# Thresholded attention into a tanh-shrink layer pair: some DMAs on the GpSimd queue, q prepared two slots sooner, and q of three pairs in four turned by the crossbar

## The chip, the cores and the metric

The kernel runs on one core of a Trainium2 chip. A core has five engines with a queue of instructions each: TensorE (PE; its weight loads are listed apart as PEld), VectorE (DVE), ScalarE (ACT), GpSimd (POOL) and SyncE (SP), which here only issues DMAs. Sixteen DMA engines move data between HBM and the core's memory SBUF and can transpose 2-byte data on the way (the crossbar). TensorE writes to PSUM. Engines run their queues in order and wait for each other by semaphores. The metric is device time in microseconds (us), the median of several runs. A profile is one execution more, recorded by the hardware.

## What is computed

```python
# q, k, v: (8, 8, 576, 64) float32; tau = 0.02; w_in (512, 2048), w_out (2048, 512)
scores = scale * np.matmul(q, k.transpose(0, 1, 3, 2))
thresh = np.max(scores, axis=-1, keepdims=True) - tau
scores = np.where(scores >= thresh, scores, -1000000000.0)
scores = scores - np.max(scores, axis=-1, keepdims=True)
attn = np.exp(scores)
attn = attn / (np.sum(attn, axis=-1, keepdims=True) + 1e-09)
attn_out = np.matmul(attn, v)
x = attn_out.transpose(0, 2, 1, 3).reshape(B * S, H * D)
h = x @ w_in
g = h - np.tanh(h)
out = g @ w_out
```

Attention over 64 (batch, head) combinations of 576 rows each, in which only scores within tau of their row's maximum count, and then two dense layers over the 4608 rows with `h - tanh(h)` between them.

## The kernel before

**Tiles and slots.** Two heads form a pair: 32 pairs `p`, four to a batch. The 2 × 576 query rows of a pair are nine tiles of 128 rows (`TPP = 9`), the ninth made of the last 64 rows of both heads, so there are 288 tiles `i`. The main loop (line 691) runs over slots `s`, one tile a slot. In slot `s` TensorE makes the scores of tile `s + 8` (`AHEAD`), ScalarE bends the scores of tile `s + 5` into `z` (`kink`, `MASK`), ScalarE takes exponentials of tile `s` (`weights`), and TensorE multiplies the weights of tile `s - 2` with v (`attend`, `LAG`). A pair's first scores thus run in slot `first = 9 p - 8`.

**What each tile does.** `scores` multiplies qT with kT and with kS (the same keys with halves swapped, so that the high and low 16-bit parts of q and k meet), 512 and 64 columns each; VectorE scales the result into SBUF and keeps the row maximum (line 336, `sc`). Each pair of tiles gets its thresholds `nb` (line 348). ScalarE makes `z` (363). For the first six pairs TensorE transposes `z` (382); from pair 6 on a crossbar DMA issued by SP does, every second tile for two tiles (line 370, `zT`). ScalarE exponentiates the turned tile (399), and `attend` uses it as weights.

**Preparation of a pair.** `load` (138) fetches k, q and v of a pair, two DMAs each, all on SP's queue (`eng = nc.sync`). `split` (181) makes a 16-bit high and low part of k and of q on GpSimd, three instructions of which the last writes `khl` or `qhl` (188). `split_v` (214) converts v on GpSimd (216 to 221). `turn` (243) transposes: for k, nine TensorE transposes into a PSUM buffer of the pool `ps_big` (which the scores use too), a VectorE copy to `kT` (258), and two GpSimd copies to `kS` (264). For q it does the same without `kS`, except where `q_by_dma(p)` is true: there one crossbar DMA on SP's queue writes qT (247). Before, that is for odd pairs from 9 on and for pair 30, thirteen in all. Buffers: two each for the raw loads, the splits, and kT, kS, qT.

**When it is issued.** `PREP` (642) lists these steps with how many slots ahead of `first` each is placed; the loop from 653 fills a table `plan`, whose steps run at the end of their slot. All is written out in one order, so a step's place fixes its place in every queue it uses:

```python
    PREP = (
        (LDK, lambda p: load(p, "k")),
        (LDK - 1, lambda p: load(p, "q")),
        (LDK - 2, lambda p: load(p, "v")),
        (8, lambda p: split(p, "k")),
        (7, lambda p: split(p, "q")),
        (5, lambda p: turn(p, "k")),
        (4, split_v),
    )
```

`LDK` is 16. The turn of k is moved to 6 slots for odd pairs and 3 for even ones from pair 5 on; q's turn comes 5 slots ahead by DMA, else 2 or 3.

**The layers.** From the second batch on, the two dense layers of the batch before run beside the attention, spread over its slots: `hidden` (493, `psH`), tanh on ScalarE (506), `g` on VectorE (512), `project` (519, `psY`). A finished block of 128 rows is copied to `yo` (532, two buffers) and stored to HBM by a DMA that SP issues (535). Each store is issued only once the next one is ready (lines 726 to 728). The last two blocks of 512 rows and the rest rows of all batches follow after the last tile.

Of the kernel before, what the change touches and what calls it, by code (L numbers as in the profile page):

```python
# [18 lines left out]
def kernel(  # L19
# [11 lines left out]
    nc = tc.nc  # L31
    P = 128

    B, H, S, D = q.shape
# [11 lines left out]
    HPAIR = H // 2  # L46
# [91 lines left out]
    def load(p, t):  # L138
        b, h0 = p // HPAIR, 2 * (p % HPAIR)
        hs = slice(h0, h0 + 2)  # L140
        src = {"k": k, "q": q, "v": v}[t]
        eng = nc.sync
        r = raws[p, t] = raw_pool.tile([P, 10, D], F32, name=f"{t}raw", tag=t)
        n = 8 if t == "v" else 10
        eng.dma_start(
            out=r[:, 0:n, :].rearrange("p (h c) d -> p h (c d)", h=2)[:, :, 0 : 4 * D],
            in_=src[b, hs, 0:512, :].rearrange("h (p c) d -> p h (c d)", c=4),
        )
        rem = src[b, hs, 512:S, :].rearrange("h s d -> s h d")
        if t == "v":  # L150
            eng.dma_start(out=r[0:64, 8:10, :], in_=rem)
        else:
            eng.dma_start(out=r[:, 4, :], in_=rem)
# [84 lines left out]

    def q_by_dma(p):

        return p >= 2 * HPAIR and (p % 2 == 1 or p == 30)

    def turn(p, t):
        hl = hls.pop((p, t))
        if t == "q" and q_by_dma(p):
            m = mats[p, t] = qk_pool.tile([P, W], FP16, name=f"{t}T", tag=t)
            nc.sync.dma_start_transpose(
                out=m.rearrange("p (c r) -> p c r", c=TPP),
                in_=hl.rearrange("p c a d -> p (c a d)"),
            )  # L250
            return
        ps = ps_big.tile([P, W], FP16, name=f"ps_{t}", tag="big")
        for c in range(TPP):
            turn_chunk(
                ps[:, c * P : (c + 1) * P], c, hl[:, c, :, :].rearrange("p a d -> p (a d)")
            )
        m = qk_pool.tile([P, W], FP16, name=f"{t}T", tag=t)
        nc.vector.tensor_copy(out=m, in_=ps)  # L258
        mats[p, t] = m
        if t == "k":  # L260
            sw = qk_pool.tile([P, W], FP16, name="kS", tag="ks")
            for lo, hi in ((0, D), (D, 0)):
                o, i = sw[lo : lo + D, :], m[hi : hi + D, :]
                nc.gpsimd.tensor_copy(out=o, in_=i)  # L264
            mats[p, "ks"] = sw
# [37 lines left out]
    def scores(i):  # L303
# [6 lines left out]
        if hh is None:  # L310
            qrem = REM
            if q_by_dma(p):
                qrem = (slice(512, 640, 2), slice(513, 640, 2))
            for n, kk in enumerate((kT, kS)):
                for dst, srcs in ((main, MAIN), (rem, REM)):
                    for hh in range(2):
                        nc.tensor.matmul(  # L317
                            out=ps[64 * hh : 64 * hh + 64, dst],
                            lhsT=qT[:, qrem[hh]], rhs=kk[:, srcs[hh]],
                            start=(n == 0), stop=(n == 1),  # L320
                        )
        else:
            lhs = qT[:, (5 * hh + t) * P : (5 * hh + t + 1) * P]
            for n, kk in enumerate((kT, kS)):
                for dst, src in ((main, MAIN[hh]), (rem, REM[hh])):
                    nc.tensor.matmul(  # L326
                        out=ps[:, dst], lhsT=lhs, rhs=kk[:, src],
                        start=(n == 0), stop=(n == 1),
                    )
# [157 lines left out]
    gs, stores = {}, []  # L487
# [29 lines left out]
    def project(m, ms, part, ps, last, cols=slice(0, d_model)):  # L517
        for n in range(4 * part, 4 * part + 4):
            nc.tensor.matmul(  # L519
                out=ps, lhsT=gs[m][:, n, ms * P : (ms + 1) * P],  # L520
                rhs=w_out_sb[:, n, cols], start=(n == 0), stop=(n == DF_C - 1),
            )
        if part == 3:
            nc_ = cols.stop - cols.start
            yo = y_pool.tile(
                [P, nc_], F32, name="yo", tag="yo" if nc_ == d_model else f"yo{int(last)}",
                bufs=2 if nc_ == d_model else 1,
            )
            if last:
                nc.scalar.copy(out=yo, in_=ps)  # L530
            else:
                nc.vector.tensor_copy(out=yo, in_=ps)  # L532
            if m < B:
                rows = out[m * S : m * S + MB, :].rearrange("(p c) n -> c p n", c=4)
                stores.append(lambda: nc.sync.dma_start(out=rows[ms], in_=yo))
            else:
                for h in range(2):
                    b = 2 * ms + h
                    eng = nc.scalar if h and nc_ < d_model else nc.sync
                    stores.append(  # L540
                        lambda b=b, h=h, eng=eng: eng.dma_start(
                            out=out[b * S + MB : (b + 1) * S, cols],
                            in_=yo[64 * h : 64 * h + 64, :],
                        )
                    )
# [8 lines left out]
    def layers(m, tail):  # L554
# [9 lines left out]
        def y_step(m, ms, part):  # L564
            if part == 0:

                odd = tail and (m, ms) > (B - 2, 1) and ms % 2 == 0
                pl, tag = (ps_o, "o") if odd else (ps_y, "y")
                ys[m, ms] = pl.tile([P, d_model], F32, name="psY", tag=tag), odd
            ps, odd = ys[m, ms]  # L570
            project(m, ms, part, ps, odd)

        def y_half(h):

            n = d_model // 2
            pl, tag = ((ps_y, "y"), (ps_o, "o"))[h]
            ps = pl.tile([P, n], F32, name="psY", tag=tag)
            for part in range(4):
                project(m, 3, part, ps, h == 0, slice(h * n, h * n + n))
# [48 lines left out]
    def w_load(piece):  # L628
# [12 lines left out]
# [7 lines that stand above are left out]
# [5 lines left out]
    for p in range(1, NPAIR):  # L653
        first = TPP * p - AHEAD
        for d, f in PREP[3 if p == 1 else 0 :]:
            d -= p == 1 and d in (3, 5)
            if d == 5 and p >= 5:
                d = 6 if p % 2 else 3
            plan.setdefault(first - d, []).append(lambda p=p, f=f: f(p))
        d = 5 if q_by_dma(p) else (2) if p >= 5 else 3 - (p == 1)  # L660
        plan.setdefault(first - d, []).append(lambda p=p: turn(p, "q"))

    load(0, "v")
# [27 lines left out]
    for s in range(-AHEAD, NTILE + LAG + 3):  # L691
        p, j = divmod(max(s, 0), TPP)
# [28 lines left out]
        if s == 0:  # L721
            nc.vector.tensor_tensor(
                out=fold, in0=ident_bf[:, 0:64], in1=ident_bf[:, 64:P], op=ALU.add
# [79 lines left out]
```

## Time and profile before

| | us |
|---|---|
| median of 3 runs (lowest, highest) | 535.39 (534.58, 536.02) |
| profiled execution, its own time | 536.14 |
| its span, first to last instruction | 534.4 |
| DMA queue of SP: share of 16 engines | 75.2% |
| v loads on SP: 32 of 256 KB, 32 of 32 KB, median to landing | 3.7 and 3.5 |
| layer stores on SP: 32 of 256 KB, median to landing | 3.1 |
| z turned by the crossbar: 117, median to landing | 3.5 |
| q turned by the crossbar: 13, median to landing | 4.1 |

A row of instructions has the line, the engine, the operation, the tile written `<-` the tiles read, shapes and a count. A number in square brackets is the time that the engine stood idle just before, with what ended it. "SPq" rows are DMA instructions in SP's queue; their duration is that of issuing, not of moving data. The granted TensorE clock was 1.00 throughout. An engine's busy share says little by itself: the share of TensorE is high all through, that of GpSimd highest in the first 66 us, and all but TensorE fall off after 460 us, where only the layers are left.

### The profile page before, as it was taken

The page shows a single profiled execution, that of the slowest core. Times are in us where ns is not written, and L with a number is a line of the kernel's source. Part 1 is how long each engine was busy: PE and PEld are TensorE (multiplying, and loading weights), DVE is VectorE, ACT ScalarE, POOL GpSimd, SP SyncE. Part 2 cuts the span into 40 slices and gives each one's busy share as a digit, 9 for nine tenths or more (in the row PEclk, how much of TensorE's full clock was granted, in tenths as well). Part 3 has the DMA queues.
Part 4 walks back from the last instruction along what each step waited for, and adds up shares of the span by engine and source line. Part 5 has one row for each costly group of instructions (what it writes and reads, how often), then busy time and mean ns, then how long its engine had stood idle before and what let it go on. Part 6 is the DMA issues. An engine that isn't in the chain of part 4 may idle for free.

```text
span 534.4 us, 12822 instructions
## 1 busy us (share of the span) xinstructions
PE 509.6 (95%) x4651; PEld 289.2 (54%) x4651; DVE 423.3 (79%) x1184; ACT 436.7 (82%) x617; POOL 289.5 (54%) x390
## 2 busy tenths in 40 slices
PE   8988899999999998989999999999999999999997
PEld 4666566555555554555555555655555555444444
DVE  5888878989989897889889898899889887554440
ACT  5999899999898988899888989899889999543330
POOL 7999987775737566574727474575747530000000
PEclk9999999999999999999999999999999999999999
DMA  7655547999996999799998999798988995401113
GB/s 203 183 186 146 182 151 186 211 163 200 173 201 146 173 189 201 151 182 195 173 199 140 213 165 210 153 188 185 207 167 178 204 148 110 104 20 41 39 40 79
DMA packets 202687, 85.32 MB, mean 160 GB/s; under 512 B 170240, under 2 KB 195072, under 8 KB 202624
## 3 DMA queue, kind: packets, MB, share of 16 engines
q1 hardware_dynamic: 202032, 84.08, 75.2%
q8 instruction: 36, 0.59, 0.5%
q10 hardware_dynamic: 592, 0.43, 0.3%
q14 instruction: 27, 0.22, 0.1%
HBM read 36.70 MB, written 9.44 MB: 86 GB/s over the span
## 4 chain that ended last, share of the span: by engine, by line
PE 64%; DVE 9%; POOL 9%; DMA 7%; ACT 6%; issue 4%; SPq 0%; POOLq 0%; ACTq 0%; DVEq 0%
PE psY L519 20%; PE psH L493 16%; PE psS L326 14%; DMA qT<-qhl 5%; PE psO L427 3%; PE psHt L493 3%; DVE sc L336 3%; DVE g L512 2%; ACT z L363 2%; POOL kS L264 2%; PE psS L317 2%; DVE yo L532 2%; PE ps_k L235 2%; ACT th L506 1%; POOL w_in_sb L626 1%
## 5 line engine op out<-in xcount | busy, mean ns | idle before, releaser
L336 DVE TENSOR_SCALAR_CACHE_REDUCE sc<-psS 128x576 f32<-128x576 f32 x288 | 214.3, 752 | 40.7 <-PE psS L326 22.0
L363 ACT ACTIVATE z<-sc,nb 128x576 bf16<-128x576 f32 x288 | 217.2, 770 | 32.5 <-DVE nb L348 30.2
L519 PE MATMUL psY<-w_out_sb,g 128*128 128x512 bf16 (+1 forms) x592 | 145.9, 374 | 0.8 <-DVE yo L532 0.8
L264 POOL COPY kS<-kT 64x1152 f16<-64x1152 f16 x62 | 70.8, 1142 | 126.3 <-DVE nb L348 124.7
L399 ACT ACTIVATE pT<-zT 128x1152 f16<-128x1152 bf16 x117 | 135.0, 1154 | 2.0 <-DMA zT<-z 2.0
L493 PE MATMUL psH<-xT,w_in_sb 128*128 128x512 bf16 x480 | 123.3, 379 | 2.3 <-DVE g L512 2.3
L326 PE MATMUL psS<-kT,qT 128*128 128x512 f16 (+1 forms) x512 | 104.4, 285 | 4.6 <-DVE qT L258 1.2
L326 PEld LDWEIGHTS <-qT 128*128 128x128 f16 x1024 | 74.2, 97 | 59.2 <-issue 5.1
L512 DVE SCALAR_TENSOR_TENSOR g<-th,psH 128x512 bf16<-128x512 f32 x128 | 87.4, 683 | 18.9 <-ACT th L506 18.6
L326 PE MATMUL psS<-kS,qT 128*128 128x512 f16 x496 | 101.4, 286 | 0.0
L506 ACT ACTIVATE th<-psH 128x512 f32<-128x512 f32 x128 | 74.7, 583 | 23.7 <-PE psH L493 23.0
L519 PEld LDWEIGHTS <-g 128*128 128x128 bf16 x592 | 51.0, 98 | 56.8 <-issue 2.4
L493 PEld LDWEIGHTS <-w_in_sb 128*128 128x128 bf16 x576 | 49.1, 98 | 57.0 <-issue 4.7
L427 PE MATMUL psO<-vb,pT 128*128 128x65 bf16 x1024 | 53.3, 194 | 0.0
L427 PEld LDWEIGHTS <-pT 128*128 128x128 f16 x1024 | 44.2, 98 | 9.7
L188 POOL TENSOR_TENSOR qhl<-qraw,qhl 128x576 f16<-128x576 f32 x31 | 39.7, 1280 | 2.6
L188 POOL TENSOR_TENSOR khl<-kraw,khl 128x576 f16<-128x576 f32 x31 | 39.7, 1280 | 2.6
L391 ACT ACTIVATE pT<-psZ 128x512 f16<-128x512 bf16 (+1 forms) x54 | 35.0, 651 | 5.0 <-PE psZ L382 4.5
L532 DVE COPY yo<-psY 128x512 f32<-128x512 f32 (+1 forms) x31 | 21.1, 681 | 14.1 <-PE psY L519 12.4
L453 DVE TENSOR_TENSOR osb<-psO,rc 128x256 bf16<-128x256 f32 x64 | 27.1, 424 | 2.2
L420 PE MATMUL psO<-vb,pT 128*128 128x130 bf16 x128 | 28.2, 220 | 0.4
L258 DVE COPY kT<-ps_k 128x1152 f16<-128x1152 f16 x31 | 23.3, 752 | 5.8 <-PE ps_k L235 5.8
(79 smaller groups left out, 516.9 us busy)
## 6 DMA issues: line engine op xcount, KB each, us to landing
vraw<-in_v_dram SPq DMA_DIRECT2D x32, 256.0 KB, 3.7
out_dram<-yo SPq DMA_DIRECT2D x32, 256.0 KB, 3.1
kraw<-in_k_dram SPq DMA_DIRECT2D x31, 256.0 KB, 3.6
qraw<-in_q_dram SPq DMA_DIRECT2D x31, 256.0 KB, 3.7
wt<-in_moe_w_in_dram SPq DMA_DIRECT2D x8, 512.0 KB, 4.7
wt<-in_moe_w_out_dram SPq DMA_DIRECT2D x8, 512.0 KB, 4.4
zT<-z SPq DMA_TRANSPOSE x117, 3.5
kraw<-in_k_dram SPq DMA_DIRECT2D x32, 32.0 KB, 3.5
```

The source lines that it names most:

```text
L188: nc.gpsimd.tensor_tensor(out=hl[:, :, 1, :], in0=x, in1=hl[:, :, 0, :], op=ALU.subtract)
L264: nc.gpsimd.tensor_copy(out=o, in_=i)
L326: nc.tensor.matmul(out=ps[:, dst], lhsT=lhs, rhs=kk[:, src], start=(n == 0), stop=(n == 1),)
L336: nc.vector.tensor_scalar(out=sc, in0=ps[:, lo : lo + S], scalar1=SC, scalar2=None, op0=ALU.mult, op1=ALU.max, accum_out=mx[:, c : c + 1],)
L363: nc.scalar.activation(out=z, in_=sc, func=ACT.Prelu, bias=nb, scale=1.0, alpha=STEEP)
L391: nc.scalar.activation(out=pt[:, off * P : (off + n) * P], in_=ps[:, 0 : n * P], func=ACT.Exp)
L399: nc.scalar.activation(out=pt[:, 0 : n * P], in_=zts.pop(i)[:, 0:n, :], func=ACT.Exp)
L427: nc.tensor.matmul(out=po[:, t - 1 + ab, :], lhsT=pt[:, blk * P : (blk + 1) * P], rhs=vb[:, hh, c, :], start=False, stop=(n == 7), skip_gr ...
L493: nc.tensor.matmul(out=ps, lhsT=w_in_sb[:, c, n * P : (n + 1) * P], rhs=xs[m][:, c, :] if m < B else xR[:, c, :, :], start=(c == 0), stop= ...
L506: nc.scalar.activation(out=th, in_=ps, func=ACT.Tanh)
L512: nc.vector.scalar_tensor_tensor(out=gs[m][:, n, :], in0=th, scalar=-1.0, in1=ps, op0=ALU.mult, op1=ALU.add,)
L519: nc.tensor.matmul(out=ps, lhsT=gs[m][:, n, ms * P : (ms + 1) * P], rhs=w_out_sb[:, n, cols], start=(n == 0), stop=(n == DF_C - 1),)
```

## The change

Four things. v loads from pair 8 on, and the layer stores of the first six blocks of 512 rows, are issued by GpSimd in place of SP. The crossbar turns q of the pairs from 8 on that aren't divisible by four, and of pair 28 (19 pairs: 9, 10, 11, 13, 14, 15, ... 27, 28, 29, 30, 31). For these pairs the splits of k and q are placed 10 and 9 slots ahead in place of 8 and 7, and q's turn 7 in place of 5. The TensorE turn of q in pairs 2 and 4 is placed 2 slots ahead in place of 3. Results don't change.

```diff
@@ -139,7 +139,8 @@
         b, h0 = p // HPAIR, 2 * (p % HPAIR)
         hs = slice(h0, h0 + 2)
         src = {"k": k, "q": q, "v": v}[t]
-        eng = nc.sync
+
+        eng = nc.gpsimd if t == "v" and p >= 2 * HPAIR else nc.sync
         r = raws[p, t] = raw_pool.tile([P, 10, D], F32, name=f"{t}raw", tag=t)
         n = 8 if t == "v" else 10
         eng.dma_start(
@@ -238,7 +239,7 @@
 
     def q_by_dma(p):
 
-        return p >= 2 * HPAIR and (p % 2 == 1 or p == 30)
+        return p >= 2 * HPAIR and (p % 4 != 0 or p == 28)
 
     def turn(p, t):
         hl = hls.pop((p, t))
@@ -532,7 +533,8 @@
                 nc.vector.tensor_copy(out=yo, in_=ps)
             if m < B:
                 rows = out[m * S : m * S + MB, :].rearrange("(p c) n -> c p n", c=4)
-                stores.append(lambda: nc.sync.dma_start(out=rows[ms], in_=yo))
+                eng = nc.gpsimd if m < B - 2 else nc.sync
+                stores.append(lambda: eng.dma_start(out=rows[ms], in_=yo))
             else:
                 for h in range(2):
                     b = 2 * ms + h
@@ -654,10 +656,12 @@
         first = TPP * p - AHEAD
         for d, f in PREP[3 if p == 1 else 0 :]:
             d -= p == 1 and d in (3, 5)
+            if d in (7, 8) and q_by_dma(p):
+                d = d + 2
             if d == 5 and p >= 5:
                 d = 6 if p % 2 else 3
             plan.setdefault(first - d, []).append(lambda p=p, f=f: f(p))
-        d = 5 if q_by_dma(p) else (2) if p >= 5 else 3 - (p == 1)
+        d = 7 if q_by_dma(p) else 3 - (p == 1 or p % 2 == 0 or p >= 5)
         plan.setdefault(first - d, []).append(lambda p=p: turn(p, "q"))
 
     load(0, "v")
```

## The prediction

> **What bounds the kernel now.** I read the engine table first, then the stretch 120 to 450 us alone, then who waits there, then single instructions. First the busy line of the page, and the stretch in which both halves of the kernel run together (start:end, then us busy on each engine, granted clock, DMA share, GB/s).
>
> ```profile
> PE 509.6 (95%) x4651; PEld 289.2 (54%) x4651; DVE 423.3 (79%) x1184; ACT 436.7 (82%) x617; POOL 289.5 (54%) x390
> ...
> 120.00:450.00 330.00, 322.96 (x2976) 181.68 (x2973) 287.99 (x818) 296.27 (x398) 187.00 (x240) 1.00 0.93 179
> ```
>
> TensorE is busy 322.96 of 330 us, ScalarE 90%, VectorE 87%, GpSimd 57%. So TensorE's own work plus its few stalls set the pace here; at most 7.04 us of stalls can be won back. The waits of that stretch (total, times, longest):
>
> ```profile
> POOL kS L264 <- DVE nb L348: 117.8, 22, 10.5
> PEld L317 <- DMA qT<-qhl: 6.1, 7, 1.7
> PE psS L317 <- DMA qT<-qhl: 3.4, 3, 1.4
> ACT pT L399 <- DMA zT<-z: 2.0, 4, 0.9
> PE psS L326 <- DMA qT<-qhl: 0.9, 1, 0.9
> ```
>
> TensorE waits for the crossbar-turned q of a new pair, and for little else. A weight load can wait while the matmul before it still streams, so the PE row counts, not PEld. Two of these stalls, in the timeline of PE, and the second seen from the SP queue:
>
> ```profile
> 206.57 0.43 PE L317 MATMUL psS<-kT,qT 128*64 128x512 f16 x4 [1.23 <-DMA qT<-qhl]
> ...
> 237.48 0.44 PE L317 MATMUL psS<-kT,qT 128*64 128x512 f16 x4 [1.43 <-DMA qT<-qhl]
> ```
>
> ```profile
> 226.13 1.30 SPq L370 DMA_TRANSPOSE zT<-z  x1
> 227.53 0.53 SPq L145 DMA_DIRECT2D kraw<-in_k_dram  x1
> 228.11 0.56 SPq L153 DMA_DIRECT2D kraw<-in_k_dram  x1
> 228.77 0.55 SPq L145 DMA_DIRECT2D qraw<-in_q_dram  x1
> 229.37 0.55 SPq L153 DMA_DIRECT2D qraw<-in_q_dram  x1
> 230.35 1.26 SPq L370 DMA_TRANSPOSE zT<-z  x1
> 231.72 2.02 SPq L247 DMA_TRANSPOSE qT<-qhl  x1
> 233.79 0.57 SPq L145 DMA_DIRECT2D vraw<-in_v_dram  x1
> 234.42 1.33 SPq L151 DMA_DIRECT2D vraw<-in_v_dram  x1
> ```
>
> q's turn is issued at 231.72, behind four loads and a z turn; the chain of waits has it landing 5.72 us later, at 237.44. TensorE stood ready at 237.48 − 1.43 = 236.05, only 4.3 us after the issue. Last, GpSimd, which will have to take the moved DMAs:
>
> ```profile
> 219.75 2.33 POOL L264 COPY kS<-kT 64x1152 f16<-64x1152 f16 x2 [10.52 <-DVE nb L348]
> ...
> 230.60 2.32 POOL L264 COPY kS<-kT 64x1152 f16<-64x1152 f16 x2 [2.94 <-DVE nb L348]
> ...
> 247.95 2.33 POOL L264 COPY kS<-kT 64x1152 f16<-64x1152 f16 x2 [7.07 <-DVE nb L348]
> ```
>
> Two pairs are 18 slots. Each copy waits for VectorE's kT (the row names what VectorE ran last): the even pair's (247.95) with 7.07 us to spare, the odd pair's (230.60) with 2.94.
>
> **What the Trainium skill says.** "DMA: Bandwidth & Descriptors", section "Issuing engines are not separate DMA queues": all issuers share the same 16 engines, and another queue saves only sequencer time. So the v loads and stores don't get cheaper for the engines, whose share is already 0.93; no run here has a GpSimd-issued transfer. The same page, "SWDGE vs HWDGE vs iDMA", says GpSimd's descriptors are written by software on its own cores, so the issue is GpSimd work; its table "Specifications" gives about 1 us to the first byte against 0.6. "SBUF — State Buffer", section "SBUF: two separate sides", warns that VectorE's 2-port modes starve that software; the long VectorE rows here (sc, g, kT) read PSUM, and by the page's "Who interferes with whom" an instruction with at most one SBUF input outside those modes doesn't contend. I count nothing for it.
>
> **The change, part by part.** A slot is 1/36 of a batch; the psY pieces of the chain repeat at 148.22, 207.25, 266.00, 324.06, 381.49, 439.26, so batches take 59.03, 58.75, 58.06, 57.43, 57.77 us and a slot 1.62.
>
> *q's turn two slots sooner.* The q split precedes it on GpSimd; the instruction orders show that GpSimd's compute sequence is the same in both kernels, so q isn't split any sooner: only SP's place moves, from after the k and q loads to before them. At the stall above the split ended at 227.66 (226.38 + 1.28); two slots before 231.72 is 228.5, so data is there, 0.8 us ahead. Landing at 228.5 + 5.7 = 234.2 is before 236.05. All stalls seen are at most 1.43, below 3.2, so all go. Their PE rows: 0.91 (at 119.78, put down there to sc, though the weight load beside it names qT), 1.23, 1.43, 0.70, 0.88: 5.15 us. Cross-check: what batches have above the shortest, 1.60 + 1.32 + 0.63 + 0.34 = 3.89, and 0.91 before them, 4.8. Bounds 3.9 to 7.0; I take **−5.0**. z turns that were behind q's wait no longer; k and q loads go 1.3 us later, with 6 slots to their split.
>
> *Six more pairs by crossbar* (10, 14, 18, 22, 26, 28; 19 against 13). Each drops nine TensorE transposes, which take 0.50 us of the chain ("PE ps_q L235 x9"): 6 × 0.50 = **−3.0**. VectorE's six 755 ns copies go too, off the path, as does one use of a ps_big buffer; bounds −3 to −5. Each adds one SP issue (1.35 us, median) and one crossbar transfer. Its engine time: plain traffic ran at 141 GB/s with share 0.49 in 40 to 54 us, so 46 MB cost about 160 us of the 402 busy (75.2%); the rest over 130 turns is 1.9 us each. Six are 11 us in 330, share 0.93 to 0.96, and 0.98 with the shorter time. Stretches of 14 us show up to 1.11, so the measure isn't full there. Their q is issued 7 slots ahead. Cost 0, bounds 0 to +4 (late z).
>
> *v loads and stores to GpSimd.* 24 pairs × 2 loads + 24 stores: 72 instructions; SP loses 48 × 0.6 + 24 × 0.54 = 42 us of issue. SP waited mostly for ScalarE's z (91.8 us), so this wins nothing itself. GpSimd pays c each. Nearest rows: SP's own 0.54 to 0.65 us; the upper bound is the roughly 2.0 us fixed part in "Anatomy of one DMA — SWDGE (gpsimd) path" of the DMA page, as if the issuer were held for all of it. I take c = 1.0. By the order, five of six DMAs in two pairs stand between the odd pair's kS and the even pair's, one ahead of the odd pair's. Five at 1.0 fit in 7.07 minus the 0.6 by which two pairs shorten, one in 2.9. Loads have 10 slots until the v split; stores aren't issued until a later row block is ready. Cost 0; if the cover goes, 5c − 7.7 us per two pairs, where 7.7 is 6.5 of idle plus 1.2 between kS's end and TensorE's first use (kT turned at 246.52, plus three slots is 251.4; kS ended 250.3).
>
> *q of pairs 2 and 4 one slot later.* Before 66 us GpSimd is 94% busy and sets the pace; TensorE stalled 0.6 us each on VectorE's qT there. Between −1.2 and +2.6; I take 0.
>
> **Sum.** −5.0 − 3.0 = −8.0. The profiled execution took 536.14 (span 534.4): 528.1. It lies 0.75 above the median 535.39, so 527.4; I say **527.5**. Late next is ScalarE, 53 of 57 us in a batch.
>
> **Rivals.**
> 1. *GpSimd late (slower).* Place: kS of even pairs, 12 times. Above c = 1.54 TensorE waits 12 × (5c − 7.7); at c = 1.67 the gain is gone; 1.8 gives 543, 2.0 gives 555. For it: two pairs already hold 17.4 us of GpSimd work in 29, and a v load is 256 pieces of 1 KB. Against it: SP's 0.6 and the page's 1 us.
> 2. *The stalls are replaced.* Fuller DMA engines delay z turns; ScalarE, with 9% to spare, passes it on. For it: zT took up to 6.9 us to land. Against: only 2.0 us of such waits today. It gives back 3 to 6 us: 530.5 to 534.
> 3. *The turn isn't sooner*, because q's split doesn't move on GpSimd and its DMAs delay it: only the −3 stays, 532.4. Against: the 0.8 us to spare at 227.66, and the even pairs' q, split by about 242.8 with three DMAs ahead, against an issue due at 243.1.
>
> **How the numbers follow.** Forecast (525 to 530.5): 0.51. Rivals 2 and 3 together (530.5 to 536): 0.23. Rival 1: 0.26, densest just past its point. No change means within 0.3%, 1.6 us, about what this kernel's timing can tell. Faster: 0.51 + 0.15 = 0.66. Same: 0.08 + 0.01 = 0.09. Slower: 0.25. Range 523 to 541: up to c = 1.76 of rival 1; the likeliest's own is 525 to 530.5.
>
> **What would show it.** qT waits on TensorE near 0; 171 − 54 = 117 ps_q matmuls; GpSimd's DMA issues near 1 us and its idle before even kS 1.5 to 2; zT's median still near 3.5; a batch near 57 us. I am wrong if kS appears as a releaser of TensorE, or if ScalarE waits for zT by more than 5 us.

## The result and the profile after

The changed kernel takes 587.68 us (median of four runs, 581.73 to 590.34) against 535.62 (534.58 to 536.02) for the kernel before: 1.096 times as long, interval 1.0874 to 1.1046. The forecast was 527.5. The profiled execution took 590.34 us, span 588.6, and its TensorE clock was granted at 0.954 on average, against 1.00 before.

First the page of the changed kernel: busy rows, clock, DMA queues, DMA issues (KB of one, median us to landing).

```profile
PE 523.3 (89%) x4535; PEld 293.9 (50%) x4597; DVE 420.6 (71%) x1178; ACT 436.6 (74%) x617; POOL 334.8 (57%) x462
...
PEclk9999999979999799979989799989979799999999
...
q1 hardware_dynamic: 195696, 72.48, 65.1%
q0 software_dynamic: 4608, 13.37, 10.2%
...
vraw<-in_v_dram POOLq DMA_DIRECT2D x24, 256.0 KB, 4.9
out_dram<-yo POOLq DMA_DIRECT2D x24, 256.0 KB, 3.6
```

The change did what it says: a second queue has appeared with 13.37 MB, the 72 new instructions stand on GpSimd (462 against 390), TensorE has 54 weight loads fewer, nine for each of six pairs. (Of its matmul records 116 are gone; 62 of these are missing from this trace, and from e1's below.) TensorE's share fell from 95% to 89%, although its busy time rose, and the clock row has dips at regular distances. The stretch 120 to 450 us, then the two windows around one dip (same columns as in the view before):

```profile
120.00:450.00 330.00, 289.42 (x2470) 160.27 (x2506) 245.09 (x696) 253.93 (x341) 204.02 (x272) 0.93 0.92 161
```

```profile
240.00:251.00 11.00, 10.95 (x109) 6.44 (x109) 10.37 (x30) 9.42 (x14) 8.22 (x12) 1.00 0.91 162
251.00:262.00 11.00, 5.91 (x49) 3.25 (x45) 4.77 (x16) 6.15 (x9) 7.67 (x12) 0.70 1.05 166
```

No engine is full over the stretch: TensorE fell from 322.96 busy us to 289.42, ScalarE from 296.27 to 253.93. The kernel isn't slower evenly. Up to 251 us TensorE is full at full clock; in the next 11 us it works 5.91 at a clock of 0.70. Who waits for what, 120 to 500 us (total, times, longest):

```profile
POOL kS L265 <- DVE nb L349: 129.9, 22, 12.0
ACT pT L400 <- DMA zT<-z: 48.6, 11, 6.0
PEld L421 <- ACT pT L400: 41.4, 12, 6.6
PE psO L421 <- ACT pT L400: 37.1, 9, 6.3
```

No wait for qT is left on TensorE. GpSimd is far from late: it idles 129.9 us before kS. What is new is ScalarE's wait for the crossbar-turned z, 48.6 us in only 11 waits, against 2.0 us before, and TensorE's wait of 37.1 us for what ScalarE makes of it.

One of these eleven is the dip at 251 us, seen from four engines, each in its own timeline: SP's queue, GpSimd, ScalarE, TensorE (start, us, then the row; the duration of a DMA row is that of issuing).

```profile
242.64 1.51 SPq L248 DMA_TRANSPOSE qT<-qhl  x1
244.20 1.27 SPq L146 DMA_DIRECT2D kraw<-in_k_dram  x1
245.53 0.56 SPq L154 DMA_DIRECT2D kraw<-in_k_dram  x1
246.13 0.59 SPq L146 DMA_DIRECT2D qraw<-in_q_dram  x1
246.77 0.55 SPq L154 DMA_DIRECT2D qraw<-in_q_dram  x1
247.41 13.12 SPq L371 DMA_TRANSPOSE zT<-z  x4
```

```profile
245.56 2.32 POOL L265 COPY kS<-kT 64x1152 f16<-64x1152 f16 x2 [2.38 <-DVE nb L349]
247.82 0.72 POOL L146 DMA_DIRECT2D vraw<-in_v_dram  x1
248.53 0.60 POOL L152 DMA_DIRECT2D vraw<-in_v_dram  x1
```

```profile
256.83 1.16 ACT L400 ACTIVATE pT<-zT 128x1152 f16<-128x1152 bf16 x1 [4.60 <-DMA zT<-z]
```

```profile
258.05 0.29 PE L421 MATMUL psO<-vb,pT 128*128 128x130 bf16 x1 [4.85 <-ACT pT L400]
```

SP issues q's turn, four loads and then a z turn at 247.41. GpSimd, done with an odd pair's kS (245.56 + 2.32 = 247.88), issues the next even pair's v load at about the same moment, 0.41 us after that z turn. From 250.95 to 256.31 us no DMA of any queue lands. The z turn takes 9.3 us, the v load 8.5; ScalarE gets its z 4.60 us late, and TensorE stands still 4.85 us. How long turns of z took to land over the whole kernel, after and then before:

```profile
DMA to landing us min/median/max: 3.2/3.7/10.7
```

```profile
DMA to landing us min/median/max: 3.2/3.5/6.9
```

The median hardly moved; a few are very late. In the records of single DMAs 31 crossbar turns after 115 us, all of z, took over 6.2 us, in 11 groups of neighbours, one for every two pairs, and in each group an even pair's v load from GpSimd was in flight. No such turn is in the kernel before over that stretch.

### The profile page after: what moved, and what is told of

Its sections match the earlier page's. It is cut to its first block, busy times and chain, and to the rows that moved or that the text cites. A ratio compares the mean times of both kernels' runs of the same rounds, so it can differ in the third digit from the quotient of the medians.

```text
span 588.6 us, 12627 instructions
## 1 busy us (share of the span) xinstructions
PE 523.3 (89%) x4535; PEld 293.9 (50%) x4597; DVE 420.6 (71%) x1178; ACT 436.6 (74%) x617; POOL 334.8 (57%) x462
## 3 DMA queue, kind: packets, MB, share of 16 engines
q0 software_dynamic: 4608, 13.37, 10.2%
## 4 chain that ended last, share of the span: by engine, by line
PE 37%; issue 17%; POOL 17%; DMA 14%; DVE 10%; ACT 4%; SPq 0%; POOLq 0%; ACTq 0%; DVEq 0%
PE psY L520 13%; PE psH L494 10%; DMA vraw<-in_v_dram 9%; PE psS L327 7%; POOL kS L265 7%; DMA zT<-z 5%; DVE g L513 3%; PE psHt L494 2%; ACT z L364 2%; DVE sc L337 2%; PE psO L428 1%; ACT th L507 1%; DVE yo L533 1%; DVE kT L259 1%; POOL khl L189 1%
## 5 line engine op out<-in xcount | busy, mean ns | idle before, releaser
L400 ACT ACTIVATE pT<-zT 128x1152 f16<-128x1152 bf16 x117 | 135.0, 1154 | 48.6 <-DMA zT<-z 48.6
L494 PE MATMUL psH<-xT,w_in_sb 128*128 128x512 bf16 x435 | 120.4, 394 | 10.2 <-DVE g L513 6.8
L327 PE MATMUL psS<-kT,qT 128*128 128x512 f16 (+1 forms) x512 | 108.6, 295 | 3.9 <-DVE sc L337 2.1
L327 PEld LDWEIGHTS <-qT 128*128 128x128 f16 x1024 | 77.3, 100 | 65.8 <-issue 13.7
L327 PE MATMUL psS<-kS,qT 128*128 128x512 f16 x496 | 105.0, 294 | 0.3
L494 PEld LDWEIGHTS <-w_in_sb 128*128 128x128 bf16 x576 | 50.5, 100 | 65.1 <-issue 15.6
L421 PE MATMUL psO<-vb,pT 128*128 128x130 bf16 x128 | 28.8, 225 | 37.1 <-ACT pT L400 37.1
L428 PE MATMUL psO<-vb,pT 128*128 128x65 bf16 x1024 | 55.1, 197 | 0.0
L428 PEld LDWEIGHTS <-pT 128*128 128x128 f16 x1024 | 46.0, 100 | 9.5 <-issue 0.6
L421 PEld LDWEIGHTS <-pT 128*128 128x128 f16 x128 | 12.6, 99 | 52.3 <-ACT pT L400 41.4
L484 DVE COPY xT<-psX 128x512 bf16<-128x512 bf16 x32 | 13.4, 420 | 34.0 <-PE psX L477 34.0
```

The costliest lines, as they stand in the source:

```text
L327: nc.tensor.matmul(out=ps[:, dst], lhsT=lhs, rhs=kk[:, src], start=(n == 0), stop=(n == 1),)
L400: nc.scalar.activation(out=pt[:, 0 : n * P], in_=zts.pop(i)[:, 0:n, :], func=ACT.Exp)
L421: nc.tensor.matmul(out=po[:, t - 1 : t + 1, :], lhsT=pt[:, 4 * P : 5 * P], rhs=vb[:, hh, 4:6, :], start=True, stop=False, skip_group_check ...
L428: nc.tensor.matmul(out=po[:, t - 1 + ab, :], lhsT=pt[:, blk * P : (blk + 1) * P], rhs=vb[:, hh, c, :], start=False, stop=(n == 7), skip_gr ...
L494: nc.tensor.matmul(out=ps, lhsT=w_in_sb[:, c, n * P : (n + 1) * P], rhs=xs[m][:, c, :] if m < B else xR[:, c, :, :], start=(c == 0), stop= ...
```

## The experiments

The theories: **G** (rival 1), GpSimd's issues make it late; **Z** (rival 2), the crossbar gets too many turns; **M**, formed on the result: v loads on a second DMA queue meet the turns, which then land late. The expectations call Z theory B, and a wider form of M theory A: packets of GpSimd's queue stretch every turn that they meet. "Before" on the same chips was 534.12 to 534.32 us.

### 1 to 4: one part at a time

The changed kernel with everything back on SP (e1_no_gpsimd), and the kernel before with only the v loads, only the stores, only the sooner turn:

```diff
# e1_no_gpsimd, from the changed kernel, in both places
-        eng = nc.gpsimd if ... else nc.sync
+        eng = nc.sync
# e2_v_only, from before
-        eng = nc.sync
+        eng = nc.gpsimd if t == "v" and p >= 2 * HPAIR else nc.sync
# e3_stores_only, from before
-                stores.append(lambda: nc.sync.dma_start(out=rows[ms], in_=yo))
+                eng = nc.gpsimd if m < B - 2 else nc.sync
+                stores.append(lambda: eng.dma_start(out=rows[ms], in_=yo))
# e4_sooner_only, from before
+            if d in (7, 8) and q_by_dma(p):
+                d = d + 2
-        d = 5 if q_by_dma(p) else (2) if p >= 5 else 3 - (p == 1)
+        d = 7 if q_by_dma(p) else (2) if p >= 5 else 3 - (p == 1)
```

> The changed kernel with every v load and store back on SP's queue; the three other parts of the change stay. Theory A (packets of GpSimd's own DMA queue fall into crossbar turns and stretch them, so z turns land late): about 527 to 529 us, ScalarE's wait for zT back to 2 to 6 us, clock 1.00. Theory B (six more turns, issued earlier, overfill the DMA engines and delay z): still above 560, zT waits still above 20 us.

> The kernel before with only the v loads from pair 8 on moved to GpSimd. Theory A: most of the loss is here, 565 to 585 us, turns that meet packets of the GpSimd queue take about 2.8 us in place of 1.3 and zT waits exceed 20 us. Theory B: 533 to 537, since neither the number of turns nor their place changes.

> The kernel before with only the 24 stores moved to GpSimd. Theory A: a loss too, smaller because there are 24 transfers in place of 48: 540 to 560 us. Theory B: 533 to 537. A third theory, that it is the two v loads per pair and their landing that count, says 535 here too.

> The kernel before with only q's splits and crossbar turn placed two slots sooner, thirteen pairs as before. My prediction's first term says 5.0 us less, 529.5 to 532, with no qT wait left on TensorE. Theory B in its other form (a q turn ahead of z turns delays these) says 536 to 545 with more zT waits.

| kernel | us (lowest, highest) | ratio to before, interval |
|---|---|---|
| e1_no_gpsimd | 533.51 (532.70, 535.96) | 0.9991, 0.9978 to 1.0003 |
| e2_v_only | 546.45 (544.54, 549.10) | 1.0237, 1.0203 to 1.0270 |
| e3_stores_only | 534.03 (532.98, 535.34) | 0.9997, 0.9987 to 1.0007 |
| e4_sooner_only | 533.50 (533.09, 534.44) | 0.9988, 0.9976 to 0.9999 |

The whole loss goes with the GpSimd queue, and alone only the v loads cost anything. That also sets the size: e1 has the rest of the change and gains almost nothing, where 527 to 529 was expected. Theory A in its wide form missed: it had e2 at 565 to 585 and e3 at 540 to 560. Of e1 the busy line of the page, and TensorE's wait for pT (120 to 450 us):

```profile
PE 505.4 (95%) x4535; PEld 286.4 (54%) x4597; DVE 419.7 (79%) x1178; ACT 436.0 (82%) x617; POOL 290.1 (55%) x390
...
PE psO L421 <- ACT pT L400: 0.4, 1, 0.4
```

The spans of after and e1 are 588.6 and 531.7, 56.9 us apart. TensorE's added wait on pT makes 36.7 of it (37.1 − 0.4), its added busy time, at the lower clock, 17.9 (523.3 − 505.4): together 54.6.

In e2 the loss sits elsewhere. Waits of e2, 120 to 450 us:

```profile
PEld L317 <- DMA qT<-qhl: 15.2, 9, 3.0
PE psS L317 <- DMA qT<-qhl: 11.5, 9, 2.7
```

With q's turn at its old, late place, it is the turn of q that comes late. TensorE waits 8.1 us longer for it than before (11.5 against 3.4). M says that any turn nearby can be hit; G would show waits for kS, and TensorE has none in this stretch.

### 5: turns and a load by themselves

A program with nothing but crossbar turns: phases of 24 turns from SP, with no load ("Alone", "Again"), or eight v loads of 256 KB from SP ("Own"), GpSimd ("Pool") or ScalarE ("Act"), or eight stores from GpSimd ("Store").

```python
for n in range(24):
    last = zt_pool.tile([P, TPP, P], BF16, name=f"zT{ph}", tag="zT")
    nc.sync.dma_start_transpose(out=last, in_=z)
    if eng is not None and n % 3 == 1:
        ...
        side(n // 3)
```

> Nothing of the attention or the layers is computed. Six phases of 24 crossbar turns of 128x1152 issued by SP, one after the other, with eight 256 KB transfers beside each: none (Alone), v loads in SP's own queue (Own), v loads issued by GpSimd (Pool), by ScalarE (Act), stores of 256 KB issued by GpSimd (Store), none (Again). Theory A: a phase alone takes 24 x 1.35 = 32 us; Own adds 8 plain transfers at about 0.9 us, 40 us; Pool and Store add what the transfers take and 1.5 us more for each turn that is met, 50 to 60 us. If it is any other ring that does it, Act is like Pool; if it is the software queue alone, Act is like Own. Theory B (the number of turns alone): Own, Pool, Act and Store within 3 us of each other.

The phases took 36.7 us (Alone), 42.2 (Own), 44.9 (Pool), 41.6 (Act), 40.9 (Store), 37.3 (Again); the 50 to 60 us of theory A did not come. Eight loads cost 5.5 us from SP, 8.2 from GpSimd. Of these 2.7 us more, most seems to be one event: from 103.4 to 108.9 us nothing landed, one turn took 8.39 us and the load beside it 7.73. It happened once in eight loads; M has an instance here, but no rule. Single turns did land late beside any second queue: the longest took 3.6 us Alone and 3.9 with SP's own loads, but 6.4 with ScalarE's and 6.3 with the stores.

### 6 and 7: combinations

e6_v_and_stores is e2 and e3 together, e7_sooner_v_stores has e4's edit as well; after differs from e7 by the six more pairs and by pairs 2 and 4.

> The kernel before with v loads and stores on GpSimd; thirteen q turns in their old place. If the DMA engines fill up: turns met by the other queue cost 1.5 us each, and once the engines are full every further one counts. Then v (+12 us) and stores (0) together give far more than +12: 560 to 580 us, zT waits of 20 us and more. If the parts simply add: 545 to 548, and the rest of the loss comes from the other parts of the change.

> As the one before, with the thirteen q turns also two slots sooner. If the DMA engines being full is all: the same as it within 5 us, and the changed kernel (19 turns) some 5 to 15 us above. If the sooner place of the q turn is what sets the software queue's loads against z turns: near 587 here already, and 546 to 550 without it.

e6: 547.56 us, ratio 1.0242 (1.0184 to 1.0300). e7: 570.62, ratio 1.0703 (1.0655 to 1.0751). So v loads and stores without the sooner turn simply add, and the edit that alone gains 0.1% costs 4.6% here. After is 9.6% above, so the rest of the change costs more again. The waits of e7, 120 to 500 us:

```profile
ACT pT L399 <- DMA zT<-z: 33.2, 12, 5.5
```

With q's turn ahead of the four loads, the z turn behind them stands beside the v load: the meeting has moved from q to z, and a late z stops ScalarE and TensorE at once.

### 8 and 9: what the two gains were worth

e8_no_q_turn is e4 with q turned neither by TensorE nor by the crossbar in the six pairs; e9_before_again is the kernel before, profiled once more.

```diff
+        if t == "q" and p in (10, 14, 18, 22, 26, 28):
+            mats[p, t] = mats[p - 1, t]
+            return
```

> Thirteen q turns two slots sooner, all on SP, and the q turns of pairs 10, 14, 18, 22, 26, 28 left out altogether: these pairs use the turned q of the pair before, so their attention is computed from another q. It prices the six TensorE turns without the crossbar turns that replace them. If TensorE sets the pace, 3 us less than the same kernel with them (533.5): 530 to 531. If the loop of ScalarE, VectorE and PSUM buffers does, within 1 us of 533.5.

> The kernel before once more, for a second profile of it. If the stalls on q's turn that I read are the rule, batches of 58 to 59 us and about 11 us of qT waits come back. If that one execution (536.14, the longest of its runs) was unlucky: batches of 57.5 us, 533 to 534.5 in all, and the kernel with q sooner is no faster because there was about 1 us to win, not 5.

e8: 531.94 us, ratio 0.9951 (0.9935 to 0.9966). Against e4's 0.9988 the six TensorE turns are worth 0.0037 × 534.3 = 2.0 us, give or take 1 by the intervals. e1, which has them on the crossbar, is at 0.9991: it loses those 2 us again. Its waits, 120 to 450 us:

```profile
ACT pT L400 <- DMA zT<-z: 7.7, 12, 1.1
PE psS L327 <- POOL kS L265: 1.9, 6, 0.3
```

In e8 ScalarE waits 4.0 us for z, so the added crossbar turns seem to delay z. But TensorE's waits for pT are no longer in e1 (0.4 us) than in e8 (0.7), so where the 2 us go isn't shown. Both kernels have the six waits for kS, one a batch; e4 has 0.3 us of them.

e9 took 534.06 us (span 532.3). Its waits for q, 120 to 450 us, where the first profile of the same kernel had 6.1 (PEld) and 3.4 (PE):

```profile
PEld L317 <- DMA qT<-qhl: 4.2, 6, 1.4
PE psS L317 <- DMA qT<-qhl: 2.6, 4, 0.9
```

Two executions of an unchanged kernel differ by about 2 us in span, and by 0.8 to 1.9 us in the stalls to be removed.

### 10 and 11: the change less one of its parts

e10_all_but_v has v back on SP and the stores on GpSimd; e11_all_but_stores the reverse. Each replaces one of the changed kernel's two conditions by `eng = nc.sync`.

> The changed kernel with the v loads back on SP; stores stay on GpSimd, 19 turns, sooner. Theory A as it stands now (v loads on the GpSimd queue and crossbar turns in flight together drop to about 100 GB/s for several us): 532 to 536, as without any GpSimd DMA. If any GpSimd DMA does it once the engines are this full: 545 to 565.

> The changed kernel with the stores back on SP; v loads stay on GpSimd. If the v loads carry it: 575 to 590. If stores and v loads are both needed (the stores hold the queue up, the loads behind them fall into more turns): 550 to 565.

e10: 536.54 us, ratio 1.0043 (1.0032 to 1.0055). e11: 547.64 (544.34 to 559.12), ratio 1.0219 (1.0171 to 1.0268, of the three runs up to 547.91). Waits of e10, then of e11:

```profile
ACT pT L400 <- DMA zT<-z: 17.0, 21, 1.8
```

```profile
ACT pT L400 <- DMA zT<-z: 25.1, 13, 4.4
```

In e10 ScalarE waits often and briefly, which costs little; in e11 seldom and long. Without v nothing of the 9.6% is left but 0.4%. But v alone gives 2.2% in this order, below both values expected of e11: stores and v loads together are worse than their sum.

### 12: is it the queue by itself?

The program of 5 with 48 turns a phase, and with the full pair of v loads (256 KB and the rest rows) as in the kernel.

```python
for n in range(48):
    last = zt_pool.tile([P, TPP, P], BF16, name=f"zT{ph}", tag="zT")
    nc.sync.dma_start_transpose(out=last, in_=z)
    if eng is not None and n % 4 == 1:
        ...
        side(n // 4)
```

> Nothing of the attention or the layers is computed. Phases of 48 crossbar turns on SP with twelve v loads beside them: both loads of a pair in SP's own queue (Own), only the 256 KB load by GpSimd (Main), both (Both), only the 32 KB load of 256-byte rows (Rem), both by ScalarE (ActBoth), none (Alone). Alone should take 48 x 1.44 = 69 us, Own about 80. If the drop to 100 GB/s comes from the small-row load, Both and Rem are long (over 95 and over 85) and Main near 83; if from the 256 KB load, Main and Both are long and Rem is not; if any second ring does it, ActBoth is as long as Both.

With the loads on SP the phase took 88.6 us, both on GpSimd 84.7, only the large one there 81.5, only the rest rows 75.1; none of the long phases expected came. The last two phases don't show what their names say: only nine of ScalarE's twelve pairs of loads were issued in full in its phase (76.1 us), and the others ran beside the turns that were to be alone (74). The tile answers, loads on SP, on GpSimd, on ScalarE:

```profile
DMA to landing us min/median/max: 3.3/3.5/3.7
```

```profile
DMA to landing us min/median/max: 3.3/4.1/7.6
```

```profile
DMA to landing us min/median/max: 2.9/3.3/5.2
```

As a rate the second queue is no loss in this program (in that of 5 it was one; each phase ran once). What it spoils is the single turn: its longest landing doubles, from 3.7 to 7.6 us. A sum or a mean over transfers can't show that.

### 13 to 15: which loads, and where

The changed kernel with GpSimd loading v of odd pairs only (e13_odd_v), of even pairs only (e14_even_v), and with the same loads on the same queue, but 6 slots ahead of the pair in place of 14 (e15_v_later).

```diff
# e13_odd_v; e14_even_v has == 0
-        eng = nc.gpsimd if t == "v" and p >= 2 * HPAIR else nc.sync
+        eng = nc.gpsimd if t == "v" and p >= 2 * HPAIR and p % 2 == 1 else nc.sync
# e15_v_later, from the changed kernel
+            if d == LDK - 2 and p >= 2 * HPAIR:
+                d = 6
```

> The changed kernel with GpSimd loading v of odd pairs alone; v of even pairs is back on SP. In the trace of the changed kernel every late z turn (over 6.2 us from issue to landing) stands beside the v load of an even pair, which GpSimd issues just after the odd pair's kS, within 0.7 us of the z turn that SP issues behind four loads. If that meeting is the cause: 533 to 538 us, no turn over 6.2 us. If it is any v load: about half of the loss, 555 to 565.

> The same with GpSimd loading v of even pairs alone, and odd pairs' v on SP. If the meeting is the cause: most of the loss, 565 to 588, late turns in every second pair. If it is any v load: 555 to 565 as in the other half.

> The changed kernel with all 48 v loads and 24 stores on GpSimd, but the v loads from pair 8 on placed 6 slots ahead in place of 14, so that GpSimd issues them after its splits and not right after kS. Same transfers, same queue, same number. If the place of the meeting is the cause: 533 to 545 us. If the queue itself is: 575 to 590 as before, or more, because v lands later.

e13: 537.37 us, ratio 1.0083 (1.0053 to 1.0112). e14: 588.5 (575.99 to 591.99, which is 1.078 to 1.108 of before; its runs lie too far apart for an interval). e15: 539.70, ratio 1.0106 (1.0085 to 1.0128). Waits, 120 to 500 us, of e13, then e14, then e15:

```profile
ACT pT L400 <- DMA zT<-z: 19.9, 20, 2.3
```

```profile
ACT pT L400 <- DMA zT<-z: 50.1, 13, 6.4
```

```profile
POOL vb L217 <- DMA vraw<-in_v_dram: 46.4, 21, 3.9
...
ACT pT L400 <- DMA zT<-z: 17.4, 19, 2.3
```

This settles where the loss arises. Beside the stores, the twelve even pairs' v loads alone make 7.8 to 10.8%, the odd pairs' 0.8%. Moving all loads to another place, with the queue, the number and the bytes as they were, takes 8.5 of the 9.6% away. So it isn't GpSimd's issue time, nor the number of DMAs, nor the six more turns: it is that the even pair's v load starts together with the z turns that stand behind q's turn and four loads on SP. e15 also shows the loads themselves late (GpSimd waits 46.4 us for v there), but a late v stops GpSimd, which has time. One mark was missed: in e13 no turn was to take over 6.2 us, but after 115 us seven did, up to 7.7.

Set side by side, the traces say more of the stores. Take the even pairs from 10 on in after, e7, e11 and e14. Where the v load began up to 0.6 us after the z turn nearest to it, 34 times, the slowest z turn in flight took 6.8 to 10.7 us to land (median 9.1). Where it began 0.3 to 0.8 us before that turn, ten times, 4.4 to 7.2 (median 6.1). In after it began later in all eleven pairs; in e11, with the stores back on SP, in four. So the stores may act through this order alone; no run moves the load by that one microsecond and nothing else. The order isn't all: in e13 seven odd pairs' loads begin after a turn, but with two or three of SP's DMAs in flight in place of four to six, and the slowest turn takes 5.3 to 7.7 us.

No version beats the kernel before by more than its timing tells: e4 and e1 are at 0.9988 and 0.9991 (e8 computes less).

## The prediction, step by step

**Which bound.** TensorE set the pace before, as read. It was taken to go on doing so; after, no engine is full.

**q's turn two slots sooner, −5.0.** The mechanism was right, the size wrong. The stalls went (no qT wait in after, nor in e4), yet e4 alone gains 0.6 us (interval 0.05 to 1.3). Two reasons can be read. The 5.15 us came from one execution; e9's has 3.5 (PE rows 2.6 and 0.9). And the cross-check, batches above the shortest, read what varies anyhow as stall: e4's batches, measured at the sc row, take 57.4 to 57.6 us without any qT wait, e9's 56.6 to 58.4 with them. Where the other 3 us of e9's stalls went isn't settled.

**Six more pairs by crossbar, −3.0 at cost 0.** The gain was 2.0 us (e8 against e4), the cost 2 us (e1 against e8), each good to about 1. The cost lies within the bounds given, 0 to +4, but the value taken was the wrong end. ScalarE's waits for z grew as rival 2 has it, but TensorE's didn't, so its place stays open. The sum also had no term for kS: once the q turns are gone, TensorE waits for it once a batch (1.9 us in e1 and in e8).

**v loads and stores to GpSimd, cost 0.** This is the step that failed. Its terms held: an issue took 0.72 us (256 KB v), 0.60 (rest rows), 0.62 (store), all below the 1.0 taken and far below the 1.54 of rival 1, and GpSimd still idles 2.38 us even before this odd pair's kS. What failed is the list of terms. I priced the move as issue time on one engine, and took for the data the sentence of the Trainium skill ("DMA: Bandwidth & Descriptors", section "Issuing engines are not separate DMA queues") that another queue saves only sequencer time. The DMA engines are shared, as it says; it also says that DMAs of different issuers interleave there, and that half was left out. On SP v stood in line with the turns, behind or ahead of them; on GpSimd it starts beside them. "Loads have 10 slots until the v split" looked at what the moved load may suffer, not at what it does to the turns: for the z turn shown ScalarE stood ready 4.8 us after its issue, and it landed after 9.3. In place of cost 0 this part took 587.68 − 533.51 = 54.2 us, with the rest of the change in place (after against e1).

**Pairs 2 and 4, 0.** Not tried alone; e1, which has it, leaves no room for more than a fraction of a per cent.

**The rivals.** Rival 1 had the right sign by the wrong path: after the first 20 us TensorE never waits for kS in after. The 0.25 given to a slower kernel therefore came true by luck. Rival 2 named the right wait ("Fuller DMA engines delay z turns; ScalarE, with 9% to spare, passes it on"), but gave it 3 to 6 us and the wrong cause: e1 has the six more turns and a fuller stretch (DMA share 0.95, after 0.92), and loses nothing. Rival 3 falls: q's turn was sooner. The prediction's own mark, ScalarE waiting for zT by more than 5 us, is what came, at 48.6.

**Multiplied by the clock.** A stall of some 5 us also lowers the granted clock after it: 0.70 in the window shown, psH matmuls at 394 ns in the mean against 379. Between its start and its end the clock record of after has eight stretches of 6.8 us at 0.50 (one is 255.5 to 262.3 us), that of e1 none. This goes with the 17.9 us of busy time above, a third of the loss, and no term of the sum had it. The Trainium skill has it ("TensorE: Matmul & The Clock Gate", section "Part 1: The HAM clock gate"): an idle window of about 3.4 us drops the array to half clock until it has been busy again. The trace agrees on the half, 0.50; a row of two psS matmuls took 0.41 us before the stall, 0.67 after it. How short a stall is enough wasn't tested.

## What to carry to other kernels

Before a DMA is moved to another issuing queue, list what it will start beside, not only what it costs its new issuer: a transfer with much slack can delay one with none. Look at the longest landing and at its neighbours in time, since neither the DMA share of the stretch nor the median showed this. A stall read from one execution of a nearly full engine need not be what its removal brings (5.15 us read, 0.6 gained); profile the unchanged kernel twice before adding such stalls up.

## What was unexpected of the hardware

From the packet records of after, in one-microsecond bins: GB/s moved, and number and mean time (ns) of the packets of 256 B in SP's queue (the turns, and the rest rows of loads) and of those of 4096 B in GpSimd's. A packet counts where it starts.

```
from us   GB/s   turn packets, ns    GpSimd packets, ns
 248       272      218     19            0      -
 249       127      423     37            4     372
 250        93      236     76            8     378
 251        83      244     63            5     552
 252       127      144     32           16     938
 253        63       62    165           11    1560
 254        42       76     50            5     249
 255       173      356     39           15     213
 256       257     1004     18            0      -
```

From 249 to 255 us, while packets of both queues are served, everything crawls, at a sixth of the rate just before at worst, and the packets of both can take many times their time. It isn't always so: in the microsecond from 257 both are served at 343 GB/s. Counting half-microsecond bins that have packets of both (those of 4 B left out) and move under 130 GB/s: after about 41 us, e14 39, e7 28, e6 and e11 14 each, e13 and e15 9 each, e2, e3 and e10 5 or less. Another way of binning shifts these by some us. The order is nearly that of the losses; e2 is the exception.

An instruction fetch lies in the same stretches: the DMA record has a queue of instruction packets, of 16 KB each, and one falls into each of the eleven groups, 0.9 to 7.1 us after the v load's start. In the kernel before, z turns beside such a packet land later too: a median of 4.8 us (29 turns after 100 us) against 3.4 (83 others). It doesn't make the loss alone, since e1 has these packets as close to the v loads, and no z turn over 5.8 us after 100 us; how much it adds isn't known.

The Trainium skill ("DMA: Bandwidth & Descriptors") says, under "Queues, rings and completion order", that each DMA engine goes round its queue rows packet by packet, and under "SWDGE vs HWDGE vs iDMA" that a packet has preferably up to 4096 B. The trace shows that size in GpSimd's queue; from SP the same v loads go in packets of 1024 and 256 B, the stores in 2048. If the packets of the record are those that the skill means, one sixteen times the turn's own in each round would slow a turn; it doesn't explain why one packet then takes 1.5 us. Three things stay open: why a load and a turn that meet crawl in some cases and not in others (once in eight loads in e5), whether the stores, which alone cost nothing, make it worse only by the order of starts (e11 against after), and whether the even pairs' v loads from ScalarE's queue would be harmless in the kernel; beside loads from that queue single turns took up to 6.4 us in e5 and 5.2 in e12. That last one wasn't tried.
